# f32 attention scores as two 64-row halves of TensorE, two more units on the f32 path, and a new order

## The chip, the cores and the metric

The kernel runs on one core of one Trainium2 chip. The metric is the device time of one execution in microseconds. The kernel before takes 719.23 us, the median of three runs (717.11 to 720.76).

## The reference

Softcapped attention feeds a two-layer block with a leaky activation. q, k and v are 4 batches x 12 heads x 448 rows x 64 columns in float32; w_in is 768 x 2048 and w_out 2048 x 768, and both arrive as float64.

```python
def _attn_ref(q, k, v, cap):
    scale = 1.0 / np.sqrt(q.shape[-1])
    scores = scale * np.matmul(q, k.transpose(0, 1, 3, 2))
    scores = cap * np.tanh(scores / cap)
    scores = scores - np.max(scores, axis=-1, keepdims=True)
    attn = np.exp(scores)
    attn = attn / (np.sum(attn, axis=-1, keepdims=True) + 1e-09)
    return np.matmul(attn, v).astype(np.float32)

def _moe_ref(x, w_in, w_out, alpha):
    h = x @ w_in
    g = np.maximum(h, 0.0) + alpha * np.minimum(h, 0.0)
    return (g @ w_out).astype(np.float32)
```

Between the two, x is the attention output with its heads side by side: 1792 rows of 768.

## The kernel before, in words

**Precision.** Most products are made of f16 pieces: an operand is split into a high and a low f16 part, and three products (two, for scores) replace one f32 product. Some of the attention of the first batches is done in f32 directly, which costs TensorE more and the other engines less.

**Attention.** Heads are worked in pairs, six pairs a batch. Batch 0 goes through `attention32`, in two parts of its rows (`PART`: 192 rows, then 256); batches 1 to 3 go through `attention`, all 448 rows at once. A unit (one pair, one part) first turns q and k by matmuls with the identity (`turn`, L483), so that the 64 dimensions of head 0 stand in partitions 0 to 63 and those of head 1 in 64 to 127, and copies them out of PSUM. For f32 scores, k of both heads then fills all 128 partitions, and q is laid out twice as long with zeros in the other head's half (`qz`): a 128-row product of a piece of `qz` with `kt` or `kz` gives the scores of one head, the zeros switching the other head off. `steps` walks over blocks of 128 score rows, two blocks a step: scores into one of two PSUM tiles `s` (L704 for batch 0, L789 for f32 scores of batch 1, L785 for split scores), tanh (L536), row maximum (L541), exp with a row sum (L548), reciprocal (L556). The exponentials are then turned, either by f32 matmuls with a diagonal of the reciprocals (`turn_32`, L595) or, split in two f16 parts, by a DMA transpose (`turn_split`, L581). `PV_32` (L648) or `PV_split` (L634) multiplies by v.

Which path a unit takes is set by numbers: `PD_A` and `PD_B` tell from which pair on batch 0 uses the DMA transpose in part 0 and part 1 (6 and 5: pair 5 of part 1 alone), `FS` which pairs of batch 1 have f32 scores (0 to 4).

**The two layers.** `w_in_chunks` and `w_out_all` load the float64 weights, make f32 of them on DVE (L906, L910, L916), and split them. `norms` (L930) finds their scales on PE. `mm1` (L810) and `mm2` (L851) are the two products of a batch, in groups of 18 matmuls a result of `mm1` and 48 of `mm2`; each needs a whole batch of attention before it.

**What sets the order.** Nothing is scheduled at run time: `Plan` records every operation with a priority and a cost for each engine that could do it (`op`), and `order` plays these costs through, engine by engine, always starting the ready operation of lowest priority number. That gives the fixed order of instructions on each engine, and for operations that several engines could do (`either`, `diff`) the engine. Penalties (`PEN`, `PEN2`, `PENP`) steer that choice, and `AQ` and `MQ` limit how many of four PSUM banks attention and the layers may hold. Where the plan sees PE with nothing ready before `FILL_END`, it puts in a matmul of the identity that nothing reads (`fill`, L1058), which costs PE its time like any other.

Of the kernel before, what the change touches and what calls it, by code (L numbers as in the profile page):

```python
# [10 lines left out]
F32 = mybir.dt.float32  # L11
# [15 lines left out]
PD_B = 5  # L27
MQ = 3
AQ = 2
PEN = 1928.88  # L30
PEN2 = 97.93
PENP = 1261.5
B0_P = -18.84
LD_P = -44.44
LO_P = -481.42
MM_P = 563.28
X_P = 17.07
ST_P = -1.38
ST1_P = 18.92
PV_P = 69.79  # L40
QK_P = -22.39
V_P = 14.66
WI_P = 64.0
WI_S = 2.76
A_S = 16.4
MM1_P = 144.38
WO_P = 177.75
WO_S = 3.92
WT_P = -550.3
WT_S = -74.76  # L50
B1_P = 63.48
B_S = 51.07
EVAC_P = -408.24
# [30 lines left out]
class Plan:  # L84
# [172 lines left out]
def kernel(  # L257
# [198 lines left out]
    def vbatch(b):  # L456
# [5 lines left out]
        u.osc, u.tok = small[:, 12 + b:13 + b], ("vam", b % 2)  # L462
        prio = V_P if b == 0 else B1_P + (b - 1) * NPAIR * B_S - B_S
# [47 lines left out]

    def steps(u, prio, n, S_, s_ns, sr_, scale, dma):

        nb = 2 * n // P
        u.sums = sums[:, u.idx % 3, :nb]
        for i0 in range(0, nb, 2):
# [8 lines left out]
            def prods(e, blocks=blocks, s=s):  # L525
                for x, c in enumerate(blocks):
                    S_(s[:, x, :S], c)

            op(pr, {"pe": sum(s_ns(c) for c in blocks)}, prods, r=sr_, w=[sr])
# [26 lines left out]
            chain(pr, (lambda r=r: nc.vector.reciprocal(out=r, in_=r),), r=[(("sums", u.idx % 3), i0, i0 + m)], w=[rt])  # L556
# [28 lines left out]
    def turn_32(u, pr, n, c, t, tr, f, fr):  # L585
# [11 lines left out]
        parts = []  # L597
        for x, rows, cols in spans(n, c):
            parts.append((x, rows, cols, [("pt", z, z + cols.stop - cols.start) for z in (u.po[x] + j * u.pitch + cols.start for j in range(NCH))]))
        if u.b == 0:  # L600
            parts = [(0, slice(0, P), slice(c * P, (c + 1) * P), [z for p_ in parts for z in p_[3]])]
        op(pr, {"pe": 4 * (P / 0.6 + 5)}, turn_P, r=[*tr, dr], w=[h, *(z for p_ in parts for z in p_[3])])
        for x, rows, cols, ptw in parts:
            op(pr, either(NCH * (rows.stop - rows.start), True), lambda e, x=x, rows=rows, cols=cols: copy(
                e, u.pt[x][:, :, cols], ps_p[h.slot][:CP].rearrange("p (j t) -> p j t", j=NCH)[:, :, rows]), r=[h], w=ptw, port=False)
# [19 lines left out]
    def PV_split(u, prio, n, vs, vt):  # L625
# [11 lines left out]
        op(prio, {"pe": 12 * (n / 2.4 + 12)}, PV, r=vt + [("pt", u.po[x], u.po[x] + 4 * n) for x in range(2)], w=[h])  # L637
        return h

    def PV_32(u, prio, n, vt, vr):  # L640
        h = plan.handle("a")

        def PV(e):
# [7 lines left out]
        op(prio, {"pe": 4 * (n / 0.6 + 30)}, PV, r=[("pt", u.po[y], u.po[y] + 4 * n) if u.b else ("pt", u.po[0], u.po[0] + 8 * n) for y in range(2)] + [vr, (vb[u.b].tok, 7, 9)],  # L651
           w=[h], rows=0.875)
# [16 lines left out]
    def attention32(part, pair):  # L669
# [4 lines left out]
        prio = A_S * (u.idx + 1) + B0_P * part  # L674
        ktr = ("tall", pair * S, (pair + 1) * S)
        if part == 0:
            h = plan.handle("a")
            rk, rkr = raw32[4, pair]
            op(prio, {"pe": 205 * NCH}, lambda e, h=h: turn(h, rk, 0, NCH), r=[rkr, identr], w=[h], rows=0.7)
            op(prio, either(S, True), lambda e, h=h: copy(e, kt[:, pair, :], ps_p[h.slot][:, :S]), r=[h], w=[ktr], port=False)  # L680
# [5 lines left out]
        qz, qr = qzs[qi][:, :2 * n], (qzr[qi][0], qzr[qi][1], qzr[qi][1] + 2 * n)  # L686
        if u.idx in (NPAIR, NPAIR + 1):
            op(prio, {"pool": 140}, lambda e: nc.gpsimd.memset(qzs[qi][D:, PART[0][1]:PART[1][1]], 0.0), w=[qzr[qi]])
        op(prio, {"pe": 205 * nch}, lambda e, h=h: turn(h, rq, c0, nch), r=[rqr, identr], w=[h, qr], rows=0.7)
        z = qz.rearrange("p (h t) -> p h t", h=2)  # L690
        for y in range(2):
            a = slice(y * D, (y + 1) * D)
            op(prio, either(n, True), lambda e, h=h, y=y, a=a: copy(
                e, z[a, y, :], ps_p[h.slot][a, o - c0 * CP:o - c0 * CP + n]), r=[h], w=[(qr[0], qr[1] + y * n, qr[1] + y * n + n)], port=False)
# [5 lines left out]
        else:  # L700
            u.po, u.pitch = [po, po + n], 2 * n
            u.pt = [pt32[:CP, po:po + 8 * n].rearrange("p (j t) -> p j t", j=NCH)]
            u.pv = [u.pt[0][:, :, y * n:(y + 1) * n] for y in range(2)]
        steps(u, prio, n, lambda s, c: nc.tensor.matmul(s, qz[:, c * P:(c + 1) * P], kt[:, pair], start=True, stop=True),  # L704
# [12 lines left out]
    def attention(b, pair):  # L717
# [52 lines left out]
        if not turn32:  # L770
            vs, vt = split_v(u, prio - 8, rv, rvt)
# [334 lines left out]
```

## Time and profile before

| | |
|---|---|
| median of three runs | 719.23 us |
| the profiled execution | 720.0 us, of which the span from first to last instruction is 717.9 us |
| PE busy | 702.5 us, 98% of the span |
| DVE, ACT, POOL busy | 497.4, 424.2 and 282.0 us |
| matmuls in the trace | 5022, each with a weight load of its own |
| `fill` matmuls in the trace | 303 |

The profile lists busy time by engine, the span in 40 slices, the chain of waits that ended last, and the costliest groups of instructions by line. A matmul's record is longer than the time it holds PE, since matmuls are pipelined; the time that one costs is the distance from its start to the next one's start. A group's busy time in the timeline overlaps the next group for the same reason, so distances between the starts of groups are what counts. An f32 matmul of the program is two records in the trace.

### The profile page before, as it was taken

The page shows a single profiled execution, that of the slowest core. Times are in us where ns is not written, and L with a number is a line of the kernel's source. Part 1 is how long each engine was busy: PE and PEld are TensorE (multiplying, and loading weights), DVE is VectorE, ACT ScalarE, POOL GpSimd, SP SyncE. Part 2 cuts the span into 40 slices and gives each one's busy share as a digit, 9 for nine tenths or more (in the row PEclk, how much of TensorE's full clock was granted, in tenths as well). Part 3 has the DMA queues.
Part 4 walks back from the last instruction along what each step waited for, and adds up shares of the span by engine and source line. Part 5 has one row for each costly group of instructions (what it writes and reads, how often), then busy time and mean ns, then how long its engine had stood idle before and what let it go on. Part 6 is the DMA issues. An engine that isn't in the chain of part 4 may idle for free.

```text
span 717.9 us, 13496 instructions
## 1 busy us (share of the span) xinstructions
PE 702.5 (98%) x5022; PEld 436.2 (61%) x5022; DVE 497.4 (69%) x965; ACT 424.2 (59%) x836; POOL 282.0 (39%) x427
## 2 busy tenths in 40 slices
PE   8999999999999999999999999999999999999997
PEld 6887878688667655554545555554555555555664
DVE  4799999899899978588988777568787602452000
ACT  5676686867788766377887565477576602331000
POOL 2433264448767643166676533256354200000000
PEclk9999999999999999999999999999999999999999
DMA  9995632668984198969887999596476810000011
GB/s 229 269 252 161 210 117 97 207 152 187 215 169 90 36 180 195 192 120 142 158 171 122 199 194 187 114 179 115 88 139 123 143 37 23 1 0 1 23 34 33
DMA packets 214336, 95.22 MB, mean 133 GB/s; under 512 B 177856, under 2 KB 210560, under 8 KB 214272
## 3 DMA queue, kind: packets, MB, share of 16 engines
q1 hardware_dynamic: 214272, 94.38, 61.8%
q8 instruction: 39, 0.64, 0.4%
q14 instruction: 25, 0.20, 0.1%
HBM read 45.82 MB, written 5.51 MB: 71 GB/s over the span
## 4 chain that ended last, share of the span: by engine, by line
PE 74%; DMA 10%; DVE 8%; ACT 4%; POOL 2%; issue 1%; SPq 0%; DVEq 0%; ACTq 0%; POOLq 0%
PE p L851 24%; PE p L810 23%; DMA ptall<-pw 7%; PE s L704 4%; PE p L634 4%; PE p L595 4%; PE s L785 3%; PE p L483 3%; PE p L648 2%; PE p L1058 2%; DMA qkTs<-nat 2%; PE p L930 1%; DVE wp L410 1%; PE s L789 1%; DVE mxs L541 1%; ACT tall L548 1%
## 5 line engine op out<-in xcount | busy, mean ns | idle before, releaser
L810 PE MATMUL p<-xring,wi 128*128 128x448 f16 (+2 forms) x1440 | 226.2, 315 | 0.0
L851 PE MATMUL p<-wp,gall 128*128 128x384 f16 x1344 | 225.0, 326 | 0.0
L810 PEld LDWEIGHTS <-wi 128*128 128x128 f16 x1440 | 135.4, 98 | 85.0 <-issue 4.3
L851 PEld LDWEIGHTS <-gall 128*128 128x128 f16 x1344 | 130.1, 98 | 89.5 <-issue 4.5
L548 ACT ACTIVATE tall<-tall,mxs,small 128x448 f32<-128x448 f32 x126 | 94.3, 750 | 18.5 <-POOL mxs L543 12.4
L820 DVE SCALAR_TENSOR_TENSOR gr<-p,ca_g,gr 128x448 f32<-128x448 f32 (+2 forms) x80 | 46.9, 586 | 55.2 <-ACT gr L400 54.8
L541 DVE TENSOR_REDUCE mxs<-tall 128x2 f32<-128x896 f32 (+1 forms) x72 | 68.5, 959 | 2.9 <-ACT tall L536 2.7
L543 POOL TENSOR_SCALAR mxs<-mxs,small 128x2 f32<-128x2 f32 (+1 forms) x76 | 39.3, 517 | 74.5 <-DVE mxs L541 59.2
L400 ACT ACTIVATE gr<-p,cs_g 128x448 f32<-128x448 f32 (+2 forms) x62 | 34.6, 557 | 53.7 <-PE p L810 50.5
L410 DVE SCALAR_TENSOR_TENSOR pw<-tall,rr,pw 128x448 f16<-128x448 f32 x63 | 47.0, 745 | 15.5 <-ACT pw L400 11.0
L407 POOL TENSOR_TENSOR pw<-tall,pw 128x448 f16<-128x448 f32 x46 | 51.6, 1122 | 15.4 <-ACT pw L394 13.5
L553 POOL TENSOR_SCALAR rr<-sums 128x2 f32<-128x2 f32 (+1 forms) x96 | 31.9, 333 | 58.4 <-ACT tall L548 31.2
L536 ACT ACTIVATE tall<-s,ams 128x896 f32<-128x896 f32 (+1 forms) x52 | 46.3, 902 | 14.3 <-PE s L785 8.6
L634 PE MATMUL p<-ptall,vs 112*64 112x448 f16 (+1 forms) x456 | 47.2, 350 | 1.4 <-DMA ptall<-pw 1.4
L400 ACT ACTIVATE wp<-p,small 128x384 f32<-128x384 f32 x19 | 10.9, 575 | 60.7 <-PE p L851 60.6
L785 PE MATMUL s<-qkTs 128*128 128x448 f16 (+1 forms) x208 | 43.0, 356 | 3.5 <-DMA qkTs<-nat 2.2
L407 POOL TENSOR_TENSOR gall<-gr,gall 128x256 f16<-128x256 f32 (+4 forms) x45 | 34.0, 761 | 29.2 <-ACT gall L394 11.6
L394 ACT ACTIVATE gall<-gr 128x384 f16<-128x384 f32 (+4 forms) x60 | 26.3, 446 | 23.2 <-DVE gr L820 23.1
L400 ACT ACTIVATE pw<-tall,rr 128x448 f16<-128x448 f32 x39 | 25.8, 661 | 22.3 <-DMA ptall<-pw 14.6
L634 PEld LDWEIGHTS <-vs 112*64 112x64 f16 x456 | 25.1, 110 | 22.8 <-issue 7.0
L407 DVE TENSOR_TENSOR gall<-gr,gall 128x384 f16<-128x384 f32 (+4 forms) x67 | 33.1, 497 | 6.0 <-ACT gall L394 3.4
L704 PE MATMUL s<-tall,qkTs 128*128 128x448 f32 x84 | 35.8, 554 | 0.2 <-ACT qkTs L394 0.2
(166 smaller groups left out, 1027.6 us busy)
## 6 DMA issues: line engine op xcount, KB each, us to landing
wp<-in_moe_w_in_dram SPq DMA_DIRECT2D x16, 768.0 KB, 6.5
wp<-in_moe_w_out_dram SPq DMA_DIRECT2D x16, 768.0 KB, 4.6
rvs<-in_v_dram SPq DMA_DIRECT2D x38, 224.0 KB, 3.1
rqk<-in_q_dram SPq DMA_DIRECT2D x18, 224.0 KB, 3.3
rqk<-in_k_dram SPq DMA_DIRECT2D x18, 224.0 KB, 3.1
ptall<-pw SPq DMA_TRANSPOSE x148, 3.3
wp<-in_k_dram SPq DMA_DIRECT2D x6, 224.0 KB, 7.7
wp<-in_q_dram SPq DMA_DIRECT2D x6, 224.0 KB, 6.0
```

The source lines that it names most:

```text
L400: nc.scalar.activation(out=o, in_=i, func=AF.Copy, scale=s)
L407: (nc.gpsimd if e == "pool" else nc.vector).tensor_tensor(out=o, in0=a, in1=b, op=ALU.subtract)
L410: nc.vector.scalar_tensor_tensor(out=o, in0=i, scalar=s, in1=hi, op0=ALU.mult, op1=ALU.subtract)
L536: op(pr, {"act": 245 + 377 * m}, lambda e, s=s, t=t, m=m: nc.scalar.activation(out=t, in_=s[:, :m, :S].rearrange("p c (j k) -> p c j k", j ...
L541: op(pr, {"dve": 136 + 469 * m}, lambda e, mt=mt, t=t: nc.vector.tensor_reduce(out=mt, in_=t, axis=AX.XY, op=ALU.max), r=tr, w=[mr], port= ...
L548: nc.scalar.activation(out=t[:, x], in_=t[:, x], func=AF.Exp, scale=capt, bias=mt[:, x:x + 1], accum_out=u.sums[:, c:c + 1])
L634: nc.tensor.matmul(pv[x * D:(x + 1) * D, :n], vs[:, z, c:c + D], u.pt[x][:CP, y * NCH + kc], start=(i == 0), stop=(i == len(prods) - 1))
L704: steps(u, prio, n, lambda s, c: nc.tensor.matmul(s, qz[:, c * P:(c + 1) * P], kt[:, pair], start=True, stop=True), lambda c: 750, [qr, kt ...
L785: nc.tensor.matmul(s[rows], qT[:, x * S + cols.start:x * S + cols.stop], qkT[:, r0:r0 + NCH, :], start=(z == 0), stop=(z == 1))
L810: nc.tensor.matmul(ps_p[h.slot][:, :n], w[:, z, kk, :], x[:, d, o:o + n], start=(kk == 0 and z == d), stop=(kk == NPAIR - 1 and z == 1))
L820: op(pr, {"dve": 198 + 1.07 * n}, lambda e: nc.vector.scalar_tensor_tensor(out=t, in0=ps_p[h.slot][:, :n], scalar=ca_g[:, j:j + 1], in1=t, ...
L851: nc.tensor.matmul(ps_p[h.slot][:, :NH], g[j][:, d, t * P:(t + 1) * P], w[:, z, hf * NH:(hf + 1) * NH], start=(j == 0 and z == d), stop=(j ...
```

## The change

The zero-padded q is gone: q of both heads is copied out of PSUM in one piece of 128 partitions. A score step no longer works on one head with 128 rows; it takes the two heads in turn, each as a 64-row matmul on its own half of TensorE's rows, with the 448 columns in two halves of 224, the heads writing to the two banks of `s`. Blocks are numbered anew, so that a step holds the same rows of both heads; where 64 rows are left over, the two heads share one block, 64 rows of PSUM each. All six pairs of batch 1 have f32 scores (`FS`), and pair 5 of part 1 of batch 0 takes the f32 turn too (`PD_B`). The unused path with f32 turns in batch 1 is removed. The plan counts 95 ns more for operations that change TensorE's mode (`TURN`, and in `TURN_P`, `SCORE`), gets other priorities and penalties, an offset for each of 156 tags (`OFF`), and lets attention hold three banks.

```diff
-PD_B = 5
+PD_B = 6
-AQ = 2
+AQ = 3
-PEN = 1928.88
+PEN = 4509.92
...
-FS = [0, 5]
-FP = [0, 0]
+FS = [0, 6]
+TURN = 95.0
+TURN_P = 905.0
+SCORE = 1040.0
...
+OFF = [34.6, 0.4, 29.9, -6.1, 0.0, 1.5, -90.6, 40.5, 0.0, 0.0, -257.7, ...]
...
-        o.prio, o.times, o.fn, o.rows, o.idx, o.port = prio, times, fn, rows, len(self.ops), port
+        o.prio, o.times, o.fn, o.rows, o.idx, o.port = prio + OFF[self.tag], times, fn, rows, len(self.ops), port
...
     def spans(n, c):
-        o = c * P
-        for h in range(2):
-            a, z = max(o, h * n), min(o + P, (h + 1) * n)
-            if a < z:
-                yield h, slice(a - o, z - o), slice(a - h * n, z - h * n)
+        i, h = divmod(c, 2)
+        if (i + 1) * P <= n:
+            yield h, slice(0, P), slice(i * P, (i + 1) * P)
+        else:
+            for h in range(2):
+                yield h, slice(h * QP, (h + 1) * QP), slice(n - QP, n)
...
+    def scores_32(qz, kz, n):
+        def prods(s, blocks):
+            for z in range(2):
+                k_ = slice(z * (S // 2), (z + 1) * (S // 2))
+                for x, c in enumerate(blocks):
+                    for y, rows, cols in spans(n, c):
+                        a = slice(y * D, (y + 1) * D)
+                        nc.tensor.matmul(s[rows, x, k_], qz[a, cols], kz[a, k_], start=True, stop=True)
+        return prods
...
-        for y in range(2):
-            a = slice(y * D, (y + 1) * D)
-            op(prio, either(n, True), lambda e, h=h, y=y, a=a: copy(
-                e, z[a, y, :], ps_p[h.slot][a, o - c0 * CP:o - c0 * CP + n]), r=[h], w=[(qr[0], qr[1] + y * n, qr[1] + y * n + n)], port=False)
+        op(prio, either(n, True), lambda e, h=h: copy(e, qz, ps_p[h.slot][:, o - c0 * CP:o - c0 * CP + n]), r=[h], w=[qr], port=False)
...
-        steps(u, prio, n, lambda s, c: nc.tensor.matmul(s, qz[:, c * P:(c + 1) * P], kt[:, pair], start=True, stop=True),
-              lambda c: 750, [qr, ktr], [icap], dma)
+        steps(u, prio, n, scores_32(qz, kt[:, pair], n), lambda blocks: SCORE, [qr, ktr], [icap], dma)
```

**The order on PE where the f32 scores of batch 1 begin.** First the kernel before. `s_61` and `s_62` are the two score tiles, `rqk` is the raw q or k, `qkTs` the turned ones, `gall` and `ptall` hold exponentials, `diags` the diagonals; a size is that of the output, and x8 stands for eight such instructions in a row.

```order
L483 MATMUL p_66<-ident,rqk 64x112 x8
L595 MATMUL p_64<-diags,gall 112x128 x4
L789 MATMUL s_62<-qkTs 128x448 x2
L789 MATMUL s_61<-qkTs 128x448 x2
L483 MATMUL p_63<-ident,rqk 64x112 x8
L595 MATMUL p_65<-diags,gall 112x128 x4
L789 MATMUL s_62<-qkTs 128x448
L789 MATMUL s_61<-qkTs 128x448 x2
L595 MATMUL p_66<-diags,gall 112x128 x4
```

Now the place where batch 1 begins in the changed kernel; `n_wi` and `mxt` belong to the maximum over all partitions that sets a weight's scale.

```order
L490 MATMUL p_64<-ident,rqk 64x112 x8
L528 MATMUL s_62<-qkTs 128x224 x4
L387 MATMUL p_66<-ident,n_wi 4x128
L612 MATMUL p_65<-diags,ptall 112x128 x4
L390 MATMUL p_66<-mxt,ones 128x4
L612 MATMUL p_63<-diags,gall 112x128 x4
L490 MATMUL p_64<-ident,rqk 64x112 x8
L612 MATMUL p_66<-diags,ptall 112x128 x4
L665 MATMUL p_65<-ptall,nat 64x256 x8
L665 MATMUL p_63<-ptall,rvs 64x256 x8
L612 MATMUL p_66<-diags,gall 112x128 x4
L528 MATMUL s_61<-qkTs 128x224 x4
```

Four score products of 448 columns, which are two steps of both heads' blocks, stood together after one turn; now a step is four products of 224 columns, and the next step stands ten rows later, between other work.

**The order on PE around a maximum for w_in's scales.** First the kernel before: between the two small matmuls of the maximum (L381 and L384) stand exponentials' turns and one of the identity matmuls.

```order
L595 MATMUL p_64<-diags,gall 112x128 x4
L381 MATMUL p_63<-ident,n_wi 4x128
L595 MATMUL p_65<-diags,gall 112x128 x4
L1058 LDWEIGHTS ident
L1058 MATMUL p_66<-ident 128x128
L384 MATMUL p_63<-mxt,ones 128x4
```

Now the same maximum (L387 and L390) for an earlier part of w_in; `wp` holds raw q and k of batch 0 there.

```order
L387 MATMUL p_65<-ident,n_wi 4x128
L490 MATMUL p_63<-ident,wp_100 64x112 x4
L490 MATMUL p_66<-ident,wp_99 64x112 x6
L528 MATMUL s_61<-tall,qkTs 128x224 x4
L390 MATMUL p_65<-mxt,ones 128x4
L528 MATMUL s_62<-tall,qkTs 64x224 x4
L612 MATMUL p_64<-diags,gall 112x128 x4
L490 MATMUL p_63<-ident,wp_99 64x112 x6
```

Between the two small matmuls stand turns of q and k and a score step instead of a matmul that nothing reads. Over the whole program the identity matmuls are 303 in the order before and 136 in the new one: 65 among the first 155 rows on PE, then none until 4 and 67 in one piece some 1,900 rows in. An instruction that needs another shape of TensorE's tiles than the one ahead of it (128 rows by 128 columns, 64 columns, 64 rows, both, or the few-row forms of a maximum) stands 203 times in the order before and 242 times in the new one.

## Rows read from the trace of the kernel before

**Rows 1.** The page: span, engines' busy time, slices of PE, DVE and clock.

```profile
span 717.9 us, 13496 instructions
PE 702.5 (98%) x5022; PEld 436.2 (61%) x5022; DVE 497.4 (69%) x965; ACT 424.2 (59%) x836; POOL 282.0 (39%) x427
PE   8999999999999999999999999999999999999997
...
DVE  4799999899899978588988777568787602452000
...
PEclk9999999999999999999999999999999999999999
```

**Rows 2.** Waits of PE over the span, longest three: us in total, times, longest.

```profile
PE s L785 <- DMA qkTs<-nat: 2.2, 2, 1.4
PE p L1058 <- POOL ident masks.py:199: 1.7, 1, 1.7
PE p L384 <- DVE mxt L377: 1.5, 2, 1.2
```

**Rows 3.** Groups on PE by shape: rows*columns of TensorE, count | busy us, mean ns.

```profile
L634 PE MATMUL p<-ptall,vs 112*64 112x448 f16 x432 | 45.7, 355 | 1.4 <-DMA ptall<-pw 1.4
L785 PE MATMUL s<-qkTs 128*128 128x448 f16 x156 | 36.6, 353 | 3.5 <-DMA qkTs<-nat 2.2 <-ACT tall L536 1.2
L704 PE MATMUL s<-tall,qkTs 128*128 128x448 f32 x84 | 35.8, 554 | 0.2 <-ACT qkTs L394 0.2
L789 PE MATMUL s<-qkTs 128*128 128x448 f32 x70 | 29.9, 549 | 1.0 <-ACT tall L536 0.9
L1058 PE MATMUL p<-ident 128*128 128x128 f16 x303 | 23.2, 229 | 1.7 <-POOL ident masks.py:199 1.7
```

**Rows 4.** Timeline of PE, 139.6 to 143.8 us: start, us, instructions.

```profile
139.77 0.99 PE L483 MATMUL p<-ident,rqk 112*64 112x112 f32 x16
140.69 1.13 PE L595 MATMUL p<-diags,gall 128*112 128x128 f32 x8
141.66 2.42 PE L789 MATMUL s<-qkTs 128*128 128x448 f32 x6
...
143.91 1.04 PE L595 MATMUL p<-diags,gall 128*112 128x128 f32 x8
```

**Rows 5.** Timeline of PE, 77 to 83 us: identity matmuls between score steps.

```profile
77.34 1.62 PE L1058 MATMUL p<-ident 128*128 128x128 f16 x26
78.80 1.72 PE L704 MATMUL s<-tall,qkTs 128*128 128x448 f32 x4
80.36 1.45 PE L1058 MATMUL p<-ident 128*128 128x128 f16 x23
```

**Rows 6.** Timeline of PE: products with v, f16 at 168 us, f32 at 64 us.

```profile
168.42 1.50 PE L634 MATMUL p<-ptall,vs 112*64 112x256 f16 x24
169.85 2.81 PE L810 MATMUL p<-xring,wi 128*128 128x192 f16 x32
...
64.64 1.52 PE L648 MATMUL p<-ptall,rvs 112*64 112x192 f32 x16
66.09 0.52 PE L930 MATMUL p<-wi 128*128 128x128 bf16 x6
```

**Rows 7.** Timeline, weight loads ahead of an f32 score step, 136.6 us.

```profile
136.56 0.30 PEld L789 LDWEIGHTS s<-qkTs 128*128 128x128 f32 x2
...
137.05 0.19 PEld L789 LDWEIGHTS s<-qkTs 128*128 128x128 f32 x1 [0.19 <-issue]
```

**Rows 8.** Stretches of 20 us: busy time of PE, PEld, DVE, ACT, POOL; clock.

```profile
20.00:40.00 20.00, 19.91 (x203) 15.84 (x203) 15.72 (x31) 13.32 (x28) 8.34 (x11) 1.00 1.01 270
80.00:100.00 20.00, 20.00 (x211) 17.25 (x210) 19.88 (x34) 14.08 (x29) 7.64 (x12) 1.00 0.37 120
220.00:240.00 20.00, 20.00 (x150) 14.26 (x149) 18.64 (x38) 17.07 (x32) 14.69 (x19) 1.00 0.27 50
580.00:600.00 20.00, 20.00 (x125) 11.53 (x122) 1.92 (x5) 3.04 (x6) 0.00 (x0) 1.00 0.07 20
```

**Rows 9.** Groups on ACT and DVE by shape: copies of q, work for split scores.

```profile
L394 ACT ACTIVATE qkTs<-p 64x448 f32<-64x448 f32 x8 | 4.3, 535 | 0.8 <-DVE qkTs L396 0.4 <-PE p L483 0.3
L364 DVE TENSOR_REDUCE small<-rqk 112x2 f32<-112x1024 f32 x13 | 15.8, 1214 | 13.3 <-DMA rqk<-in_q_dram 11.0 <-DMA rqk<-in_k_dram 2.4
```

More of the change, by code (lines that the diff above doesn't have):

```diff
@@ L26 @@
 PD_A = 6
-PD_B = 5
+PD_B = 6
 MQ = 3
-AQ = 2
-PEN = 1928.88
[L31 to L53, printed above, removed]
+AQ = 3
+PEN = 4509.92
+PEN2 = -1345.18
+PENP = 6482.25
+B0_P = -50.35
+LD_P = -35.85
+LO_P = 301.38
+MM_P = 3324.02
+X_P = 53.71
+ST_P = 19.81
+ST1_P = 13.45
+PV_P = 374.14
+QK_P = -32.7
+V_P = -1.09
+WI_P = 40.03
+WI_S = -0.97
+A_S = 13.05
+MM1_P = 198.89
+WO_P = 329.05
+WO_S = -16.5
+WT_P = -1461.61
+WT_S = -141.91
+B1_P = 277.05
+B_S = 241.79
+EVAC_P = -145.66
 LAT = 35.0
@@ L523, in steps @@
             pr = prio + (ST1_P if u.b else ST_P) * i0
[L525 to L529, printed above, removed]
+            op(pr, {"pe": s_ns(blocks)}, lambda e, blocks=blocks, s=s: S_(s, blocks), r=sr_, w=[sr])
             if u.b == 0:
@@ L595, in turn_P @@
                 nc.tensor.matmul(ps_p[h.slot][:CP, j * P:(j + 1) * P], t[:, j], d, start=True, stop=True)
[L597 to L605, printed above, removed]
+        parts = list(spans(n, c))
+        ptw = [("pt", z, z + cols.stop - cols.start) for x, _, cols in parts for z in (u.po[x] + j * 2 * n + cols.start for j in range(NCH))]
+        x, _, cols = parts[0]
+        o, i = u.pt[:, :, x * n + cols.start:x * n + cols.stop], "p (j t) -> p j t"
+        if len(parts) == 2:
+            o, i = u.pt.rearrange("p j (h t) -> p j h t", h=2)[:, :, :, cols], "p (j h t) -> p j h t"
+        op(pr, {"pe": TURN_P}, turn_P, r=[*tr, dr], w=[h, *ptw])
+        op(pr, either(NCH * P, True), lambda e: copy(
+            e, o, ps_p[h.slot][:CP].rearrange(i, j=NCH, t=P // len(parts))), r=[h], w=ptw, port=False)
     def split(prio, raw, rr_, sv, st, hi, hr, lo, lr, direct):
@@ L674, in attention32 @@
         prio = A_S * (u.idx + 1) + B0_P * part
+        plan.tag = 3 * u.idx
         ktr = ("tall", pair * S, (pair + 1) * S)
@@ L721, in attention @@
         prio = B1_P + ((b - 1) * NPAIR + pair) * B_S
+        plan.tag = 3 * u.idx
         n = 2 * NCH * D
@@ L726, in attention @@
         load(prio - 20, rk, k, b, pair, [rkr])
-        scores32, turn32 = (b == 1 and x[0] <= pair < x[1] for x in (FS, FP))
+        scores32 = FS[0] <= u.idx - 2 * NPAIR < FS[1]
         qkT = qkTs[:, u.idx % 2]
@@ L779, in attention @@
-        qT = qkT.rearrange("p g t -> p (g t)")
-        def S_(s, c):
-            for z in range(2):
-                for x, rows, cols in spans(S, c):
-                    r0 = 2 * NCH * (1 + z) + x * NCH
-                    nc.tensor.matmul(s[rows], qT[:, x * S + cols.start:x * S + cols.stop], qkT[:, r0:r0 + NCH, :],
-                                     start=(z == 0), stop=(z == 1))
-        if scores32:
-            steps(u, prio, S, lambda s, c: nc.tensor.matmul(s, qz[:, c * P:(c + 1) * P], kz, start=True, stop=True),
-                  lambda c: 750, [qt], [icap], not turn32)
-        else:
-            steps(u, prio, S, S_, lambda c: 590 if c == 3 else 380, [qt], [sc, amt], not turn32)
@@ L800 @@
+        if scores32:
+            steps(u, prio, S, scores_32(qz, kz, S), lambda blocks: SCORE, [(qt[0], 0, 2 * S)], [icap], True)
+        else:
+            steps(u, prio, S, split_scores, lambda blocks: 760 if len(blocks) == 2 else 590, [qt], [sc, amt], True)
+        plan.tag = 3 * u.idx + 2
+        h = PV_split(u, prio + PV_P, S, vs, vt)
+        xout(u, prio + PV_P, h, S, 0, 1 / P_TOP)
     grn = [0]
@@ L1014, in out_scale @@
     def out_scale(b):
+        plan.tag = -1
         def scale(e):
@@ L1022, in mm1_batch @@
     def mm1_batch(b, o, n, part):
+        plan.tag = 146 + b + (1 if b else part)
         for j in range(NF):
@@ L1026, in mm2_batch @@
     def mm2_batch(b):
+        plan.tag = 151 + b
         x = 0
```

77 lines of the change are left out of this document (35 added, 42 removed).

## The prediction, on record before the changed kernel ran

> **What bounds the kernel now.** I read the page first. PE is busy for 702.5 of 717.9 us, and its slices are nines nearly to the end [rows 1]. Busy time alone says little, since records overlap, so I looked next at what PE waits for: the three longest waits add up to 5.4 us over the whole span [rows 2]. From 580 us on no other engine has more than a few microseconds of work in 20 [rows 8]; the end of the program is PE's queue alone. So PE's queue sets the time, and every microsecond taken out of it counts if the other engines keep up. In the front they hardly do: DVE is busy 19.88 of the 20 us from 80 on, and 18.64 from 220 on [rows 8]. That is the second limit, and my main doubt.
>
> Three things fill PE's queue besides useful products: the identity matmuls (303 records [rows 3]), the changes of tile shape, and the few waits. The sum below goes through the queue, so I need PE's price of a column. Six f32 records of 448 columns run from 141.66 to 143.91 us [rows 4]: 0.375 us each, 0.84 ns a column and record. An f16 record needs half of that: 24 of 256 columns take 1.43 us to the next group's start [rows 6], in pairs, 12 x 256 x 0.42 ns = 1.29 us, and 0.14 us is left over for the change of shape.
>
> **The scores.** They are 84 + 70 records of 448 columns before [rows 3]; 154 x 0.375 = 57.8 us, all at full width. After, the order holds 192 products of 224 columns, so 384 records of 0.188 us. One after another they would take 72.2 us, and two by two 36.1 us. No row of this trace has a product on 64 rows, so this is bounded from both sides by other rows. The nearest are the products on 64 columns, f32 as well and also with two heads taking turns: 16 records of 112 columns of L483 take 0.92 us from 139.77 to 140.69 [rows 4]. One by one they would take 16 x 112 x 0.84 = 1.51 us, in pairs 0.75. L648 says the same at 192 columns: 1.45 us [rows 6], against 2.58 one by one and 1.29 in pairs. So column halves run in pairs. I take row halves to do so too, because the heads alternate instruction by instruction as they do there, and write to different banks in 36 of 48 steps. **Term: -21.7 us**; the other end is +14.4.
>
> A step now loads weights eight times instead of four. Two f32 loads ahead of a step together take 0.30 us where one takes 0.19 [rows 7], so they start 0.11 us apart. If the loads of the two halves queue behind each other, a step takes 8 x 0.11 = 0.88 us instead of 4 x 0.188 = 0.75, and 48 steps take 6 us more. Loads on column halves show no such limit (16 of them within 0.92 us), so I count nothing and keep the 6 us for the range.
>
> **The changes of shape.** They go from 203 to 242 in the order. L483 takes 0.17 us more than its pairs, and the eight records of L595 behind it take 0.97 us up to 141.66, where 8 x 128 x 0.84 = 0.86 would do [rows 4]. A detour into another shape costs 0.28 us, 0.14 for each change. **Term: 39 x 0.14 = +5.5 us.** If the new shape has to show a whole f32 weight load (0.19 us [rows 7]) at each change, it is 2 us more.
>
> The Trainium skill has the rule that changing the tiling mode drains TensorE (TensorEngine Tiling (Array Packing), Key Properties); the 0.14 us is what this trace shows of it, and the sum stands by that number.
>
> **The two pairs on the f32 path.** Pair 5 of batch 1 gets 32 more records of L483 (two groups, 2 x 0.75 = +1.5 us) and loses 16 f16 score products (12 full ones of 0.188 and 4 in pairs, -2.6 us). Pair 5 of part 1 of batch 0 gets four more turns of L595 (4 x 0.86 = +3.4 us) and a product of L648 at 256 columns (8 pairs x 256 x 0.84 = +1.7 us), and loses 24 records of L634 (-1.3 us [rows 6]). **Term: +2.7 us.** Both units take work off the others: a 1.21 us maximum over q and k on DVE [rows 9], the splits, and five DMA transposes.
>
> **The identity matmuls.** There are 167 fewer; 26 of them fill 77.34 to 78.80 us [rows 5], 56 ns each: 9.4 us of PE's queue. They stood where the plan saw nothing ready, so not all of it is time: taking them out only helps where real work now stands there. The order shows that it does (a score step and turns between the two matmuls of a maximum), but what the other engines have not delivered, PE will wait for. With nothing to say which, I count half. **Term: -4.7 us**, bounds 0 and -9.4.
>
> **The other engines.** One copy of q instead of two saves 0.3 to 0.55 us for each of 17 units (L394 at 448 columns takes 535 ns [rows 9]), on ACT or DVE. Counting DVE's order, each row by the mean of its form in the trace, gives records of 545 us before and 540 after, ACT 444 and 441, POOL 287 and 269. I cost all of this at nothing, since PE's queue covers it. Without that cover it is the first rival's.
>
> **The sum.** -21.7 + 5.5 + 2.7 - 4.7 = -18.2 us. The profiled execution took 720.0 us, 2.1 us outside its span and 0.8 above the median of the runs. 720.0 - 18.2 = 701.8, and against the median 719.2 it is 701.0. **I forecast 701 us.** With the identity matmuls at either bound, 6 us for loads and 2 us for changes, the forecast's own range is 694 to 711.
>
> **Rivals.**
>
> *DVE holds the front.* PE's queue gets shorter, DVE's hardly does (540 for 545). If DVE sets when the exponentials and weights of the front are ready, only its own 5 us come off, and PE waits for the rest: 714 us. For it speaks DVE's 19.88 of 20 [rows 8]; against it, that products of the two layers stand among those of attention in the order, ready to fill PE, and that DVE has 1.4 us of slack in 20 at 220. It decides once DVE is busy over 19.5 of 20 us through the front and PE waits over 10 us on it. 0.14.
>
> *Row halves do not run together.* Then the scores cost 72.2 instead of 36.1 us, PE's sum is -18.2 + 36.1 = +18, and the time 737 us; the full gain of the identity matmuls would bring it to 732. This is the case on the other side, and it begins to be slower when the two halves overlap by less than half. For it: no row shows the shape. Against it: the pairs on column halves. 0.07.
>
> *The leftover steps run one by one.* In 12 of the 48 steps both heads write to the same bank, 64 partitions each. If they take turns there, each costs 8 x 0.188 instead of 4 x 0.188, and 12 x 0.75 = 9 us are lost: 710 us. On column halves two products share a bank in different partitions and do run in pairs [rows 4], which speaks against it; that they differ in rows as well speaks for it. 0.09.
>
> The Trainium skill states that different row tiles cannot access the same PSUM bank at the same time (TensorEngine Tiling (Array Packing), Restrictions and Gotchas). By that rule this rival would be the forecast; no run here shows it yet.
>
> *Pairs are imperfect everywhere.* Loads queue (+6 us), or the two passes of an f32 product make a step five slots long instead of four (48 x 0.188 = +9 us): 707 to 710 us. 0.09.
>
> *The new order waits in places of its own*, or the clock, granted in full throughout [rows 1], falls to 1.2 GHz in a stretch that the identity matmuls kept filled, which doubles the cost of the products there: 716 to 726 us. 0.06.
>
> **How the numbers follow.** The forecast keeps 0.55. Its own range and the two cases of 707 to 711 lie inside 690 to 716, and so does most of the DVE case; serial halves and a bad order lie outside. Low end: all identity matmuls gained (-4.7 us) and the first pair's work off DVE shortening some waits, 701 - 11 = 690. A difference of 0.5%, 3.6 us, is about what a measurement of this kernel can tell from none. Faster by more than that means under 715.6: the forecast 0.55, both imperfect pairings 0.18, most of the DVE case 0.11, together 0.84. Within 0.5%: the rest of the DVE case and half of the bad order, with a little of the others, 0.08. Slower: serial halves and the rest, 0.08.
>
> **What would show it.** Right: two L528 records of different heads start within 0.02 us of each other and the next two 0.19 us later; a two-block step takes 0.75 us and 0.1 to 0.4 us of changes; PE's records of the scores sum to some 36 us of its queue; waits of PE stay under 15 us. Each rival has its own mark: starts 0.19 us apart one by one (serial); that in the 64-column steps alone (shared bank); starts 0.22 us apart (loads); PE waiting on DVE or ACT in the front; a granted clock under 1.00 before 690 us. The forecast is wrong if the pairs are there and the time is still over 711: then the gain went into waits, and the waits of PE name them.

## The result, and the profile after

The changed kernel takes 694.89 us (median of 4 runs, 694.19 to 696.31) against 718.92 for the kernel before beside it (717.11 to 720.76): a ratio of 0.9668, 95% interval 0.9639 to 0.9698. It is 24.0 us faster. The forecast was 701.0 us, range 690 to 716: inside, and 6.1 us short of the gain. The profiled execution's span went from 717.9 to 694.5 us.

The page of the kernel after, with the lines of [rows 1]:

```profile
span 694.5 us, 13601 instructions
...
PE 680.4 (98%) x5122; PEld 433.6 (62%) x5122; DVE 486.9 (70%) x953; ACT 420.7 (61%) x828; POOL 265.0 (38%) x405
...
PE   8999999999999998999999999999999999999997
...
DVE  4899999999989987786886858588688503441000
...
PEclk9999999999999999999999999999999999999999
```

PE is full as before, and the clock reads 1.00 in every stretch of 20 us up to 680. PE's busy time fell by 22.1 us, nearly the 23.4 that the span lost. DVE lost 10.5 us, twice the 5 that the prediction had counted, and its nines in the first third stand closer together.

Groups on PE by shape in the kernel after (count | busy us, mean ns | idle before, releaser), to hold against [rows 3]:

```profile
L528 PE MATMUL s<-qkTs 64*128 64x224 f32 x144 | 18.5, 375 | 0.0
L528 PE MATMUL s<-tall,qkTs 64*128 64x224 f32 x144 | 17.7, 371 | 0.0
L528 PE MATMUL s<-tall,qkTs 64*64 64x224 f32 x48 | 5.8, 362 | 0.0
L528 PE MATMUL s<-qkTs 64*64 64x224 f32 x48 | 5.8, 362 | 0.0
...
L1063 PE MATMUL p<-ident 128*128 128x128 f16 x136 | 10.7, 241 | 3.1 <-DVE xring L416 1.5 <-POOL ident masks.py:199 1.4 <-DVE gr L816 0.2
```

The 384 records of the scores replace 154 full ones. A record's own duration (370 ns) counts the overlap twice; what matters is how far apart groups start. Timeline of PE after, three places (start, us, instructions): a step that shares one bank, a two-block step, and two two-block steps in a row:

```profile
19.62 0.97 PE L528 MATMUL s<-tall,qkTs 64*64 64x224 f32 x8
20.52 0.38 PE L390 MATMUL p<-mxt,ones 1*128 1x1 f32 x2
...
37.40 1.03 PE L528 MATMUL s<-tall,qkTs 64*128 64x224 f32 x8
38.36 0.34 PE L926 MATMUL p<-wi 128*128 128x128 bf16 x3
...
53.23 1.78 PE L528 MATMUL s<-tall,qkTs 64*128 64x224 f32 x16
54.94 0.55 PE L665 MATMUL p<-ptall,rvs 112*64 112x192 f32 x4
```

Eight records take 0.90, 0.96 and (half of 1.71) 0.86 us to the next group. One by one they would take 8 x 0.188 = 1.50, in pairs 0.75. They run in pairs, in the shared bank too. Read record by record, the eight of the step at 37.40 start 0, 7, 293, 300, 483, 489, 672 and 678 ns after its start, and the next group at 958: two and two, 7 ns apart. Only the first pair takes longer, 0.29 us instead of 0.19.

Distances between starts, added up by kind over PE's whole queue, give the ledger (us; a product counted at 0.84 to 0.85 ns a column in f32, half of that in f16 and bf16, and half again for pairs):

| | before | after | difference | in the sum |
|---|---|---|---|---|
| products | 651.3 | 632.4 | -18.9 | -21.7 + 2.7 = -19.0 |
| identity matmuls | 16.9 | 7.6 | -9.3 | -4.7 |
| changes of shape | 29.4 | 35.1 | +5.7 | +5.5 |
| waits and ends | 20.4 | 19.4 | -1.0 | 0 |
| span | 717.9 | 694.5 | -23.4 | -18.2 |

Longest waits of PE after (us in total, times, longest), to hold against [rows 2]:

```profile
PE s L785 <- ACT tall L553: 2.2, 2, 1.8
PE p L490 <- DMA wp<-in_k_dram: 1.6, 2, 1.2
PE p L1063 <- DVE xring L416: 1.5, 1, 1.5
```

The waits sum to some 10 us in either kernel. The ledger's first two lines are counts at those prices; what the trace adds is that little else moved, the changes by +5.7 and the waits by -1.0. So three of its four lines came as predicted, and the fourth, the identity matmuls, came off the queue in whole. Stretches of 20 us (PE, PEld, DVE, ACT, POOL, clock), first three of after, then two of before that are not in [rows 8], show what stands where they stood:

```profile
40.00:60.00 20.00, 20.00 (x209) 16.30 (x207) 19.77 (x36) 17.03 (x34) 9.04 (x13) 1.00 0.79 246
60.00:80.00 20.00, 20.00 (x221) 16.91 (x220) 19.88 (x35) 18.55 (x43) 8.29 (x15) 1.00 0.93 270
...
120.00:140.00 20.00, 20.00 (x225) 16.49 (x222) 19.87 (x35) 15.20 (x35) 10.03 (x15) 1.00 0.92 229
```

```profile
40.00:60.00 20.00, 19.84 (x221) 16.13 (x219) 17.88 (x42) 14.53 (x33) 7.45 (x12) 1.00 0.76 219
...
120.00:140.00 20.00, 20.00 (x151) 13.22 (x151) 18.16 (x27) 15.51 (x33) 7.04 (x12) 1.00 0.67 233
```

DVE gives away 0.1 to 0.2 us of 20; in the two stretches of before it gave away 2 (0.8 in the one between, and 0.1 from 80 to 100 us [rows 8]). Up to the end of attention of batch 1, first before and then after (columns as above, DVE third):

```profile
0.00:301.10 301.10, 294.45 (x2583) 214.60 (x2583) 257.45 (x481) 213.74 (x429) 147.39 (x219) 1.00 0.73 173
```

```profile
0.00:285.30 285.30, 277.27 (x2705) 214.57 (x2705) 254.77 (x482) 217.42 (x439) 144.03 (x216) 1.00 0.76 182
```

DVE is busy for 257.5 of 301.1 us before and 254.8 of 285.3 after: 2.7 us less work, and 13 us less idle time. So 15.8 of the 23.4 us are won by then. The other 7.6 come later: 3.4 in attention of batches 2 and 3, and 4.2 behind its end, where a smaller rest of the two layers is left (137.6 us before, 133.4 after).

### The profile page after: what moved, and what is told of

The parts are those of the page before. It is cut to its first block, busy times and chain, and to the rows that moved or that the text cites. A ratio compares the mean times of both kernels' runs of the same rounds, so it can differ in the third digit from the quotient of the medians.

```text
span 694.5 us, 13601 instructions
## 1 busy us (share of the span) xinstructions
PE 680.4 (98%) x5122; PEld 433.6 (62%) x5122; DVE 486.9 (70%) x953; ACT 420.7 (61%) x828; POOL 265.0 (38%) x405
## 4 chain that ended last, share of the span: by engine, by line
PE 80%; DMA 9%; DVE 5%; ACT 3%; issue 2%; POOL 1%; SPq 1%; ACTq 0%; DVEq 0%; POOLq 0%
PE p L847 29%; PE p L806 24%; PE p L612 6%; DMA ptall<-pw 5%; PE s L785 5%; PE p L651 5%; PE s L528 4%; PE p L665 3%; PE p L490 2%; DMA wp<-in_moe_w_out_dram 2%; PE p L926 1%; DMA qkTs<-nat 1%; DMA nat<-in_v_dram 1%; DVE mxs L558 1%; PE p L390 1%
## 5 line engine op out<-in xcount | busy, mean ns | idle before, releaser
L558 DVE TENSOR_REDUCE mxs<-tall 128x2 f32<-128x896 f32 x72 | 68.4, 960 | 11.5 <-ACT tall L553 11.2
L560 POOL TENSOR_SCALAR mxs<-mxs,small 128x2 f32<-128x2 f32 (+1 forms) x68 | 30.4, 448 | 86.9 <-DVE mxs L558 81.3
L570 POOL TENSOR_SCALAR rr<-sums 128x2 f32<-128x2 f32 x96 | 35.2, 367 | 51.8 <-ACT tall L565 35.0
L651 PE MATMUL p<-ptall,vs 112*64 112x448 f16 x432 | 45.5, 354 | 1.7 <-DMA ptall<-pw 1.2
L553 ACT ACTIVATE tall<-s,ams 128x896 f32<-128x896 f32 (+1 forms) x48 | 42.3, 901 | 6.1 <-PE s L785 3.5
L413 POOL TENSOR_TENSOR pw<-tall,pw 128x448 f16<-128x448 f32 x35 | 39.8, 1137 | 13.3 <-ACT pw L400 11.0
L785 PE MATMUL s<-qkTs 128*128 128x448 f16 (+1 forms) x192 | 38.1, 355 | 2.7 <-ACT tall L553 2.2
L406 ACT ACTIVATE pw<-tall,rr 128x448 f16<-128x448 f32 x43 | 28.5, 663 | 15.6 <-DMA ptall<-pw 11.9
L612 PE MATMUL p<-diags,gall 128*112 128x128 f32 x280 | 36.0, 278 | 0.5 <-POOL diags L408 0.5
L402 POOL CAST gall<-gr 128x192 f16<-128x192 f32 (+4 forms) x32 | 22.7, 711 | 34.6 <-DVE gr L816 33.9
```

The costliest lines, as they stand in the source:

```text
L406: nc.scalar.activation(out=o, in_=i, func=AF.Copy, scale=s)
L413: (nc.gpsimd if e == "pool" else nc.vector).tensor_tensor(out=o, in0=a, in1=b, op=ALU.subtract)
L553: op(pr, {"act": 245 + 377 * m}, lambda e, s=s, t=t, m=m: nc.scalar.activation(out=t, in_=s[:, :m, :S].rearrange("p c (j k) -> p c j k", j ...
L558: op(pr, {"dve": 136 + 469 * m}, lambda e, mt=mt, t=t: nc.vector.tensor_reduce(out=mt, in_=t, axis=AX.XY, op=ALU.max), r=tr, w=[mr], port= ...
L612: nc.tensor.matmul(ps_p[h.slot][:CP, j * P:(j + 1) * P], t[:, j], d, start=True, stop=True)
L651: nc.tensor.matmul(pv[x * D:(x + 1) * D, :n], vs[:, z, c:c + D], u.pt[x][:CP, y * NCH + kc], start=(i == 0), stop=(i == len(prods) - 1))
```

## The experiments

Three readings were to be told apart. **Queue:** the time follows PE's own queue, so the pairs bring 16 us net and identity matmuls and waits the rest. **DVE and order:** in the front PE and DVE wait for one another, and a shorter queue pays only with an order that has work ready. **Clock and cover:** identity matmuls hold something up, and taking them out costs.

| | median us | ratio to before, 95% interval | to the kernel after, us |
|---|---|---|---|
| e1_heads_in_turn | 694.83 | 0.966 (0.9642 to 0.9678) | -0.1 |
| e2_before_few_identity | 719.45 | 1.0009 (0.9991 to 1.0027) | (edit of before) |
| e3_dve_longer | 706.32 | 0.982 (0.9802 to 0.9838) | +11.4 |
| e4_no_offsets | 708.07 | 0.9842 (0.9825 to 0.986) | +13.2 |
| e5_half_again | 708.44 | 0.9849 (0.9817 to 0.9881) | +13.6 |
| e6_scores_twice | 726.31 | 1.0089 (1.006 to 1.0119) | +31.4 |
| e7_full_width_new_order | 711.2 | 0.9884 (0.9854 to 0.9913) | +16.3 |
| e8_halves_old_order | 715.62 | 0.9945 (0.993 to 0.9961) | (edit of before) |
| e9_dve_shorter | 693.01 | 0.964 (0.9609 to 0.9672) | -1.9 |
| e10_two_copies | 697.82 | 0.9701 (0.9675 to 0.9727) | +2.9 |
| e11_late_identity_out | 698.24 | 0.9707 (0.9649 to 0.9766) | +3.3 |
| e12_two_units_back | 726.26 | 1.0114 (1.0083 to 1.0146) | +31.4 |

The last column is a difference of medians; the kernel before's own median moved by up to 0.8 us between the chips used.

**e1: the two products of a head behind one another.**

```diff
-            for z in range(2):
-                k_ = slice(z * (S // 2), (z + 1) * (S // 2))
-                for x, c in enumerate(blocks):
...
+            for x, c in enumerate(blocks):
+                for y, rows, cols in spans(n, c):
+                    a = slice(y * D, (y + 1) * D)
+                    for z in range(2):
...
```

> The changed kernel with one edit: inside a step the two 224-column halves of one head come first, then those of the other head, so neighbours in the queue share their half of TensorE's rows. Same products, same order of everything else on every engine. If PE's queue sets the time and only the taking of turns lets products run in pairs, a step needs seven or eight slots of 0.188 us instead of four, 0.56 to 0.75 us more for each of 48 steps: 694.9 + 27 to 36 = 722 to 731 us. If DVE holds the front and PE has slack there, under 10 us come on: below 705 us. If the hardware pairs the halves whatever their order, nothing changes: 695 us.

Measured 694.83 us, the same. Timeline of PE in e1, one two-block step and the next group:

```profile
36.85 1.03 PE L528 MATMUL s<-tall,qkTs 64*128 64x224 f32 x8
37.81 0.52 PE L926 MATMUL p<-wi 128*128 128x128 bf16 x6
```

0.96 us again. Record by record, the eight start 0, 14, 294, 307, 483, 496, 672 and 685 ns after the step's start: two and two again, though now the first head's two products stand ahead of the second head's in the program. So the pairs do not come from the order of the loops, as the prediction had argued ("because the heads alternate"). That each half takes its own products as they come is the likely reading; the records do not name the head, so which two products make a pair is not shown.

**e2: the order before, 32 of 303 identity matmuls issued.**

```diff
+    fill_no = [0]
...
-        for _ in range(FILLS):
+        fill_no[0] += 1
+        for _ in range(FILLS if fill_no[0] <= 32 else 0):
```

> The kernel before with its order untouched, except that only the first 32 of the 303 identity matmuls are issued. 271 of them at 56 ns are 15.2 us of PE's queue. If PE's queue sets the time even there, 719 - 15 = 704 us. If half of them only covered waiting, as the prediction's sum had it, 711 us. If they all stood where PE had nothing to do, 719 us, and PE's waits grow by 15 us. If the granted clock falls in the front without them, slower than 719.

Measured 719.45 against 719.1 us: nothing gained from 271 x 56 ns = 15.2 us of matmuls. PE of e2 over the place of [rows 5], and then the waits of PE of e2 up to 100 us:

```profile
77.06 1.77 PE L704 MATMUL s<-tall,qkTs 128*128 128x448 f32 x4 [2.31 <-ACT qkTs L394]
80.36 1.77 PE L704 MATMUL s<-tall,qkTs 128*128 128x448 f32 x4 [1.53 <-ACT gall L536]
```

```profile
PE s L704 <- ACT qkTs L394: 3.8, 3, 2.3
...
PE s L704 <- ACT gall L536: 1.5, 1, 1.5
```

Ahead of these two score steps PE waits 2.31 and 1.53 us for ACT. In the kernel before, identity matmuls stood in this place, and its waits for the copies of q in the first 100 us summed to 0.2 us. Over the span PE's waits rise from 10.4 to 23 us. The matmuls were covers of waits, mostly for ACT and DVE, and cost nothing by themselves. In this run the granted clock stays at 1.00 from 60 to 80 us with PE busy for only 15.42 of 20. That does not hold for every run: in five of the ten the mean clock of the span is 0.995 to 0.997, and the median of these five is 720.2 us against 718.2 for the others, so some of what was saved may go into the clock there.

**e7: the new order, scores at full width.**

```diff
...
-                        nc.tensor.matmul(s[rows, x, k_], qz[a, cols], kz[a, k_], start=True, stop=True)
+            for x, c in enumerate(blocks):
+                cols = list(spans(n, c))[0][2]
+                nc.tensor.matmul(s[:, x, :S], qz[:, cols.stop - P:cols.stop], kz, start=True, stop=True)
```

> The changed kernel with its order, but each score block as one product of 128 rows and 448 columns again, without the zeros (so it adds the two heads' scores: a part of the computation is wrong in it and the time is read for the order alone). 84 blocks take 63.0 us instead of 36.3, and 53 changes of tile shape go (242 to 189), at 0.15 to 0.2 us 8 to 10.6 us: 16 to 19 us more of PE's queue. If the row halves bring the gain, 711 to 714 us. If the new order alone brings it, 695 to 700 us.

Groups on PE of e7 by shape:

```profile
L525 PE MATMUL s<-qkTs 128*128 128x448 f32 x84 | 35.7, 550 | 0.0
L525 PE MATMUL s<-tall,qkTs 128*128 128x448 f32 x84 | 35.6, 552 | 0.0
```

Measured 711.2 us. 168 records of 448 columns are 63.0 us of queue instead of 36.3, and the changes of shape fall from 242 to 189: 26.7 - 53 x 0.15 = +18.8 us of queue for +16.3 us of time. In the new order the halves bring about 16 us; order, merged copies and the two moved units together bring the other 8. Under order come the table of offsets, the penalties and the third bank for attention; of these only the table is taken out by itself (e4).

**e8: the order before, halves in batch 0 alone.** The order is that of before, q stays padded with zeros, and batch 0's steps take of q and k only the 64 partitions that belong to a head. The blocks of batch 0 are numbered as in the changed kernel.

```diff
...
+                if u.b == 0:
+                    S_(s, blocks)
+                    return
...
+        def halves(s, blocks):
+            for z in range(2):
...
```

> The kernel before with its order, instruction by instruction, and only the scores of batch 0 as row halves (q stays zero-padded and copied twice; batch 1 as before). 42 blocks of 0.75 us become 24 steps of 0.75: 13.5 us less, and 28 more changes of shape (203 to 231) take 4 to 5.6 us back. If PE's queue sets the time from the start, 719 - 8.5 = 710.5 us. If PE has room in the first 95 us, as the run without identity matmuls showed, only what lies behind counts, 8.2 of 35.8 us of these scores by the stretches of the profile: 717 to 719 us.

Measured 715.62 us, -3.7. PE of e8 by shape:

```profile
L725 PE MATMUL s<-tall,qkTs 64*128 64x224 f32 x144 | 18.0, 372 | 0.1
L725 PE MATMUL s<-tall,qkTs 64*64 64x224 f32 x48 | 6.2, 362 | 0.0
```

Batch 0's scores fall from 84 x 0.375 = 31.5 us to 192 records in pairs, 96 x 0.188 = 18.0, and 28 more changes take back 28 x 0.14 = 3.9: 9.6 us less of queue, of which 3.7 arrive by the medians. The result lies between the two readings, 710.5 and 717 to 719. The profiled run is the fastest of the ten, 713.90 us: its span is 6.1 us shorter than before, and PE's waits sum to 13.1 us instead of 10.4. So some of the shorter queue ends in waits in the old order, where the 303 identity matmuls stand as they stood. Another part may be the clock: the three longest runs (716.80 to 717.87 us) have a mean of 0.996 or 0.997.

**e4: the new list of operations, without its table of offsets.**

```diff
-OFF = [34.6, 0.4, 29.9, -6.1, 0.0, 1.5, -90.6,
...
+OFF = [0.0] * 156
```

> The changed kernel with every entry of the table of offsets at 0; the rest of the plan as it is. The order then holds 331 identity matmuls instead of 136 and 250 changes of tile shape instead of 242, for the same products: PE's queue is 10.9 + 1.2 us longer. If PE's queue sets the time, 694.9 + 12 = 707 us. If the order buys nothing and the halves alone do, 695 us. If the table also spares waits on other engines, over 710 us.

Measured 708.07 us, +13.2. The order then holds 331 identity matmuls and 250 changes of shape, PE's first product of the layers starts at 127.2 us instead of 85.5, and attention of batch 1 ends at 292.4 instead of 285.3. With the plan's other numbers as they are, more than half of the gain hangs on this table, that is on where the new products are put. A plan made without the table could have chosen those other numbers differently, so this is no measure of the best order without it.

**e3 and e9: DVE longer, DVE shorter.** e3 takes one more quarter of a row maximum in the 48 score steps of batches 0 and 1:

```diff
...
+                if u.b < 2:
+                    nc.vector.tensor_reduce(out=mt, in_=t[:, :, :1], axis=AX.XY, op=ALU.max)
...
```

> The changed kernel with one more maximum on DVE in each of the 48 score steps of batches 0 and 1, over a quarter of the step's elements, ahead of the full one; the order does not know of it. By the rows of the full maximum (0.96 us for 896 elements, 0.62 for 448) it is about 0.45 us in two-block steps and 0.37 in the others, some 20 us of DVE's queue, estimated. If PE alone sets the time, DVE's slack takes most of it: 695 to 701 us. If DVE sets the front as tightly as PE, which its 19.4 to 20.0 us of 20 from 40 to 140 us hint at, 706 to 715 us.

e9 takes only that quarter there:

```diff
-                out=mt, in_=t, axis=AX.XY, op=ALU.max), r=tr, w=[mr], port=False)
+                out=mt, in_=t[:, :, :1] if u.b < 2 else t, axis=AX.XY, op=ALU.max), r=tr, w=[mr], port=False)
```

> The changed kernel with the row maximum of batches 0 and 1 taken over a quarter of the step's columns alone, which leaves part of the computation out and is read for the time: by the rows of the run with a longer DVE (0.37 us for a quarter, 1.08 for all in two-block steps) some 36 x 0.7 + 12 x 0.35 = 29 us come off DVE's records in the front. If PE's queue is the bound there now, 690 to 695 us. If DVE still holds the front by as much as the run with more DVE says (0.68 us a us), 675 to 680 us.

Two stretches and the whole front, up to the end of attention of batch 1, of e3, and then of e9 (columns as above):

```profile
60.00:80.00 20.00, 18.02 (x197) 15.46 (x193) 19.79 (x38) 17.36 (x38) 6.99 (x13) 1.00 0.80 245
...
100.00:120.00 20.00, 17.76 (x174) 13.62 (x172) 19.79 (x40) 18.20 (x35) 14.09 (x23) 1.00 0.25 78
...
0.00:295.10 295.10, 278.62 (x2703) 213.68 (x2705) 271.45 (x531) 219.02 (x440) 142.95 (x216) 1.00 0.72 176
```

```profile
60.00:80.00 20.00, 20.00 (x217) 16.79 (x216) 17.25 (x35) 18.56 (x42) 8.84 (x16) 1.00 0.84 257
...
100.00:120.00 20.00, 20.00 (x185) 16.26 (x182) 17.91 (x35) 19.38 (x43) 12.13 (x19) 1.00 0.28 87
...
0.00:281.70 281.70, 276.83 (x2704) 214.48 (x2705) 231.75 (x482) 217.01 (x439) 137.51 (x216) 1.00 0.77 184
```

In e3 DVE does 16.7 us more up to the end of batch 1 (271.5 for 254.8), two of PE's four stretches from 40 to 120 us fall to 18 of 20, PE's waits sum to 18 us instead of 10, and the time rises by 11.4. In e9 DVE does 23 us less and gives 2 to 3 us of each 20 away, PE's stretches are full, and the time falls by 1.9 us, less than its interval can tell from nothing. DVE has hardly any room left upward, and downward it no longer holds anything: the two engines stand level, and with DVE's work cut it is PE's queue that is left.

**e5 and e6: more of PE.** e5 computes the first 224 columns of each score step a second time, e6 all of them.

```diff
-            for z in range(2):
+            for z in (0, 1, 0):
```

> The changed kernel with the first 224 columns of every f32 score step computed once more, both heads, into the same place: two more slots of 0.188 us in each of 48 steps, 18 us of PE's queue in the stretch up to 285 us. The order does not know of it. If PE's queue sets the time there, 694.9 + 18 = 713 us. If DVE holds the front and PE has room, 695 to 702 us. If both bind, as the run with a longer DVE hints (11.4 us for 16.7 us more of DVE up to the end of batch 1), 703 to 709 us.

```diff
-            for z in range(2):
+            for z in (0, 1, 0, 1):
```

> The changed kernel with every f32 score step computed twice: four more slots in each of 48 steps, 36 us of PE's queue, as much as the row halves would cost if they did not run in pairs. If PE's queue sets the time, 694.9 + 36 = 731 us, which would be slower than before. If PE has some room in the front, 715 to 725 us. If DVE alone holds the front, under 705 us.

Measured +13.6 us for 48 x 2 x 0.188 = 18.0 us of queue, and +31.4 for 36.1. As far as PE's queue goes, e6 is what the changed kernel would be if the halves ran one behind the other: 726.31 us, slower than before, by a ratio of 1.0089. The first 18 us cost three quarters of themselves, the next 18 all: the slack of PE's queue in the front is some 4 us.

**e10: q copied in two pieces, as before.**

```diff
...
+            for a in (slice(0, D), slice(D, P)):
+                copy(e, qz[a], ps_p[h.slot][a, o - c0 * CP:o - c0 * CP + n])
...
```

> The changed kernel with the turned q copied out of PSUM in two pieces of 64 partitions, as before, back to back on the same engine: 18 more copies, 13 on ACT and 5 on DVE, of 0.32 to 0.62 us, some 7.5 us in all; order and PE's products untouched. If the merged copy is worth something of its own, 1 to 4 us: 696 to 699 us. If PE's queue covers it, 695 us. If ACT and DVE hold the front, up to 701 us.

Measured 697.82 us, +2.9. The four runs of e10 (from 697.45) lie above the four of the kernel after (to 696.31), but the two intervals of the ratio overlap, so the size is uncertain. A copy of 128 partitions takes 529 ns and one of 64 takes 535 [rows 9], so each merged one saves a whole copy. Copies of q on ACT in the kernel after:

```profile
L400 ACT ACTIVATE qkTs<-p 128x448 f32<-128x448 f32 x6 | 3.2, 529 | 0.0
```

**e11: the last 71 identity matmuls left out.**

```diff
...
+        for _ in range(FILLS if fill_no[0] <= 65 else 0):
```

> The changed kernel with its last 71 identity matmuls, which stand in two runs around 210 us, not issued; 4.0 us of PE's queue, order untouched. In the kernel before, 271 of them cost nothing. If these too only fill waiting, 695 us. If they hold back what stands behind them, 691 us.

Measured 694.80, 695.28, 701.21 and 702.15 us: no gain, and two runs some 7 us longer. Stretches of 5 us of the kernel after, and then of e11 in the run of 694.80:

```profile
210.00:215.00 5.00, 4.60 (x69) 3.68 (x66) 4.97 (x10) 3.24 (x5) 3.35 (x4) 1.00 0.33 98
215.00:220.00 5.00, 3.95 (x36) 2.77 (x36) 5.00 (x7) 3.38 (x5) 2.74 (x2) 1.00 0.21 39
```

```profile
210.00:215.00 5.00, 2.58 (x17) 1.06 (x14) 5.00 (x9) 2.74 (x5) 3.93 (x3) 1.00 0.31 84
215.00:220.00 5.00, 3.66 (x14) 1.69 (x14) 5.00 (x7) 3.88 (x6) 1.85 (x1) 0.67 0.28 52
```

DVE is busy almost without a break here (the split of the second layer's weights), and PE waits for it. Without the matmuls PE is idle for half of 210 to 215 us, and from 215 to 220 us the granted clock averages 0.67: part of that stretch runs at 1.2 instead of 2.4 GHz. In the two longer runs the mean clock of the span is 0.990, in the shorter two 0.996. The 0.006 between them is 4.2 us of 700, which would be some two thirds of the 6.6 us that the two pairs of runs lie apart. This is an estimate from the mean clocks, since the longer runs left no trace; where their clock fell is not known.

**e12: the two moved units put back on the path of before.**

```diff
-PD_B = 6
+PD_B = 5
...
-FS = [0, 6]
+FS = [0, 5]
```

> The changed kernel with pair 5 of part 1 of batch 0 and pair 5 of batch 1 back on the f16 paths (PD_B and FS as before); the plan makes a new order from this, with offsets that were not made for it. PE's products take 5.6 us less by the count of its order, DVE's records 11 us more, and the order holds 510 identity matmuls instead of 136. If PE's queue alone sets the time, 689 us. If DVE matters as in the run with a longer DVE, 0.68 us a us, 694.9 - 4 + 7 = 698 us. If the order is the worse for the offsets as well, as without the table (+13 us), 702 to 712 us; then the two units' own worth stays open.

Measured 726.26 us. The numbers of the table of offsets belong to one list of operations; with another list the planner, given the same table, leaves 510 identity matmuls and new waits. Longest waits of PE in e12:

```profile
PE s L785 <- DMA qkTs<-nat: 5.1, 6, 2.9
PE p L651 <- DMA ptall<-pw: 3.4, 3, 2.0
```

The clock has a part in it too. Its mean is 0.988 in this run and 0.991 to 0.995 in the other three, and it is at the lower of its two levels behind the wait of 2.0 us for the DMA of `ptall`:

```profile
460.00:465.00 5.00, 3.86 (x21) 1.95 (x17) 3.70 (x9) 2.70 (x7) 1.31 (x4) 0.50 1.09 222
```

This says nothing of what the two units are worth, which stays open. It shows only that this table does not serve another list of operations.

## Why the prediction was right, and where it was short

**The pairs.** The mark it named (starts within 0.02 us, the next two 0.19 later) is there: 7 ns, then 0.29 us to the second pair and 0.19 to the third and fourth. At 0.189 us a pair the 192 pairs of the scores take 36.3 us of the queue for 36.1. The reason given, that heads alternate, was not the cause (e1): the pairs came for another reason, which was luck. The serial rival, on the other side, would have come true by 726 us (e6) and not 732 to 737: of the 11 us to 737, 6 are the forecast's own distance from the result, and nearly 5 are hidden by the slack of PE's queue in the front.

**The shared bank.** The 12 steps take 0.90 us, less than the two-block steps, so this rival falls. By the rule of the Trainium skill that different row tiles cannot access the same PSUM bank at the same time (TensorEngine Tiling (Array Packing), Restrictions and Gotchas) they would take 1.5 us; where the two write different partitions of the bank, as here, the trace does not agree.

**Loads and changes.** Loads of the halves do not queue: later pairs are 0.19 apart, not 0.22. The first pair of a two-block step takes 0.10 us more. That the first load stands in the open there is a reading, not shown; the 0.10 us lies in the +5.7 us of the changes, predicted at +5.5.

**The two units.** The products' line, -18.9 for -19.0, bears the +2.7 us out as far as counts at these prices go; their effect on the other engines was not settled (e12).

**The identity matmuls: the term that was mis-sized.** It was counted at half, -4.7; -9.3 came off the queue. The reason given, that taking them out only helps where real work stands, was right, but the half was a guess, and read from PE alone. e2 shows that the matmuls themselves were worth nothing: they stood over waits, mostly for ACT and DVE. Whether their time is won is decided by those engines, and there the prediction costed all changes at nothing. In fact DVE's idle time up to the end of batch 1 fell by 13 us, with PE's waits no longer: the merged copies (about 2.9 us by e10) and the table (13.2 us by e4) probably have their part in that; how the 13 us divide is not shown. These are no terms to add to the 16 us of the halves, since each run takes one part out of the finished whole: the order without halves brings 8 us (e7), halves in batch 0 in the old order 4 of 10 (e8), all together 24.

**The DVE rival.** Half of its mark appeared, DVE above 19.5 of 20 from 40 to 140 us; the other half, PE waiting over 10 us on it, did not. Its reasoning, that only 5 us come off if DVE sets the front, took DVE's idle 43.6 us of before (301.1 less 257.5) for fixed. It was a margin, and the new order used 13 us of it. e3 shows how near the rival was: 17 us more on DVE give 706.

**The clock** stayed at 1.00; e11 shows that the rival had its place at 215 us, where the new order keeps 67 identity matmuls.

**The range.** The forecast's own range of 694 to 711 does not follow from its terms, which give 701 - 4.7 = 696 and 701 + 4.7 + 6 + 2 = 714. The result lies just below the lower of these, and inside the stated 690 to 716, whose low end counted on the whole of the identity matmuls and on shorter waits.

No run here beat the changed kernel by more than its interval while computing the same.

## What to carry to other kernels

Two products that fill half of TensorE's rows each can replace a zero-padded full one at half the price, even in f32 and, where they write different partitions, in one PSUM bank, if each shape change (here 0.14 us) is paid for. Filler on a full engine is not a cost to be halved: look at what stands behind each wait it covers, because its time comes back only as far as the engine waited for gets faster or is asked earlier. When two engines stand level, sum both queues and count the idle time of the second as a reserve that a new order can spend.

## What the runs showed of the hardware that was not expected

- Products on 64 rows ran in pairs with the heads alternating and with two products of one head behind one another alike: 7 ns (after) and 13 or 14 ns (e1) between the two starts of a pair, 0.96 us a step in both.
- Two row halves that write 64 partitions each of one bank lose nothing by it: 0.90 us for eight records, against 0.96 in the steps on two banks.
- The first pair of a two-block step takes 0.29 us to the next pair's start, the later ones 0.19.
- With PE busy for 2.58 of 5 us and 3.66 of the next 5, the granted clock averaged 0.67 in the second (e11); with 15.42 of 20 busy it stayed at 1.00 (e2, 60 to 80 us, in the profiled run).
